# Attention with q/k norm, then a squared-ReLU feed-forward: pair 0's exponentials ahead of the weights, half of q's norm product on ScalarE, one weight tick moved to the next stage, the last pair summed from its parts

## The chip, the core and the metric

The kernel runs on one core of a Trainium2 chip. The metric is the device time of one execution in microseconds (us), lower is better. Times of the kernel before and after are medians of several executions; the profile is that of one execution.

The engines have their own queues of instructions and wait for each other by semaphores: TensorE (PE in the profile; its weight loads are PEld), VectorE (DVE), ScalarE (ACT), GpSimd (POOL) and SyncE (SP, which issues the transfers).

## The reference

Eight batches, twelve heads, 448 positions, head size 64. q and k are normalised by their root mean square and multiplied by gains; then softmax attention; the heads' outputs side by side make 3584 tokens of 768, which go through a feed-forward of 768 to 2048 to 768 with a squared ReLU.

```python
def rmsnorm(x, g):
    rms = np.sqrt(np.mean(x * x, axis=-1, keepdims=True) + 1e-06)
    return x / rms * g
q_n, k_n = (rmsnorm(q, g_q), rmsnorm(k, g_k))
scores = scale * np.matmul(q_n, k_n.transpose(0, 1, 3, 2))
scores = scores - np.max(scores, axis=-1, keepdims=True)
attn = np.exp(scores)
attn = attn / (np.sum(attn, axis=-1, keepdims=True) + 1e-09)
attn_out = np.matmul(attn, v)
# x: (B, H, S, D) -> (B*S, H*D)
h = x @ w_in
r = np.maximum(h, 0.0)
return ((r * r) @ w_out)
```

The weights arrive as float64 and are turned into float32 on the chip.

## The kernel before

A pair is two heads of one batch. There are 48; the work goes in four spans of two batches (twelve pairs). The first twelve pairs' attention runs alone (attention_alone); the later spans' attention runs among the second products of the span before. The two products of the feed-forward are block products with seven multiplications in place of eight, whose sums and differences of weight blocks (S1 to S4) are made once, during attention_alone and the first product of span 0, and written to DRAM.

Each engine's instructions come in the order in which this program writes them (manual_schedule). So each statement below also says what stands behind what in a queue.

**The norm of a pair.** Squares on ScalarE, sums on VectorE, the power -1/2 and the product with q on GpSimd. k is not multiplied: its factor goes into the exponential as a scale. normalise_in_turn is the form for pair 1, with q and k apart and the product on VectorE.

```python
def normalise_in_turn(nc, raw, sq, rstd, mhalf, between=lambda: None):
    SP, _, n = rstd.shape
    for s in range(2):
        nc.scalar.activation(sq[:, s], raw[:, s], AF.Square)  # L332
        nc.vector.tensor_reduce(rstd[:, s], sq[:, s].rearrange("p (n d) -> p n d", n=n), AX, ALU.add)  # L333
        nc.vector.tensor_scalar(rstd[:, s], rstd[:, s], float(n) / sq.shape[2], 1e-6, ALU.mult, ALU.add)  # L334
        nc.gpsimd.tensor_tensor(rstd[:, s], rstd[:, s], mhalf[:SP, 0:n], ALU.pow)  # L335
        if s == 0:
            between()
            nc.vector.tensor_tensor(sq[:, 0].rearrange("p (j h d) -> p h j d", j=n // 2, h=2),  # L338
                                    raw[:, 0].rearrange("p (h j d) -> p h j d", j=n // 2, h=2),
                                    rstd[:, 0].rearrange("p (h j) -> p h j ()", h=2)
                                    .to_broadcast([SP, 2, n // 2, sq.shape[2] // n]), ALU.mult)

def norm(i):
    if i >= NAT:
        squares(i)
        return norm_by_squares(i)
    raw, sq = (places_of(qk, i, n)[:SP] for n in range(2))
    rstd = rstds[i] = small.tile([SP, 2, 2 * NJ], F32, tag="rstd", name="rstd", bufs=4)
    normed[i] = sq[:, 0], raw[:, 1]
    if i == 1:
        return normalise_in_turn(nc, raw, sq, rstd, mhalf)
    nc.scalar.activation(sq, raw, AF.Square)  # L698
    nc.vector.tensor_reduce(rstd, sq.rearrange("p s (n d) -> p s n d", d=D), AX, ALU.add)  # L699
    nc.vector.tensor_scalar(rstd, rstd, 1.0 / D, 1e-6, ALU.mult, ALU.add)  # L700
    flat = rstd.rearrange("p s n -> p (s n)")
    nc.gpsimd.tensor_tensor(flat, flat, mhalf[:SP, 0:4 * NJ], ALU.pow)  # L702
    nc.gpsimd.tensor_tensor(sq[:, 0].rearrange("p (j h d) -> p h j d", j=NJ, h=2),  # L704
                            raw[:, 0].rearrange("p (h j d) -> p h j d", j=NJ, h=2),
                            rstd[:, 0].rearrange("p (h j) -> p h j ()", h=2).to_broadcast([SP, 2, NJ, D]),
                            ALU.mult)
```

**One pair's scores, values and total.** The exponentials are on ScalarE (L759). The sum over keys is made by adding the first three tiles of exponentials on VectorE (add_up), and multiplying that sum and the fourth tile with ones on TensorE (total_of). finish divides, and combine_x makes the sums of xT that the first product takes as operands (its second group reads xC[:, 1]).

```python
def transpose(i, s, n):
    pt = bank("pt", n)
    for j in range(NJ):
        nc.tensor.transpose(pt[:, j * SP:(j + 1) * SP], normed[i][s][:, j * P:(j + 1) * P], ident[:SP, :SP])  # L742
    if s:
        nc.scalar.copy(qkT[:, i % 2, s], pt)  # L744
    else:
        nc.scalar.activation(qkT[:, i % 2, s], pt, AF.Copy, scale=gains[:, 0:1])  # L746
# ...
def scores(i, c):
    at = i % 2 if i < NAT else 0
    sc = ps_s.tile([SP, 2, 512], F32, tag="s", name="sc")
    for h in range(2):
        rows = slice(h * D, (h + 1) * D)
        nc.tensor.matmul(sc[:, h, 0:S], qkT[rows, at, 1, c * SP:(c + 1) * SP], qkT[rows, at, 0, :],  # L754
                         start=True, stop=True)
    pr = probs[i, c] = places[(NJ * i + c) % len(places)][:SP]
    if i < NAT:
        for h in range(2):
            nc.scalar.activation(pr[:, h], sc[:, h, 0:S], AF.Exp, scale=rstds[i][:, 1, 2 * c + h:2 * c + h + 1])  # L759
# ...
def add_up(i, c):
    acc = acc_of(i)[:SP]
    nc.vector.tensor_tensor(acc, probs[i, 0] if c == 1 else acc, probs[i, c], ALU.add)  # L769
# ...
def values(i, chunks=range(NJ)):
# ...
        pavs[i] = ps_o.tile([P, S], F32, tag="o", name="pav") if i >= NAT or i % 2 == 0 else bank("pav", 1)
    for c in chunks:
        for h in range(2):
            nc.tensor.matmul(pavs[i][h * D:(h + 1) * D, :], vs[i][:, h, c, :], probs[i, c][:, h, :],  # L810
                             start=(c == 0), stop=(c == NJ - 1))
def total_of(i):
    tots[i] = ps_o.tile([P, S], F32, tag="t", name="tot")
    for n, pr in enumerate((acc_of(i)[:SP], probs[i, NJ - 1])):
        for h in range(2):
            nc.tensor.matmul(tots[i][h * D:(h + 1) * D, :], sums["ones"], pr[:, h, :],  # L819
                             start=(n == 0), stop=(n == 1))
# ...
def finish(i):
    b, hp = divmod(i, NPAIR)
    pav, factors = pavs.pop(i), xT[:, b % 2, hp]
    x = factors
    if i < NAT:
        turned, factors = sums["turned"], sums["factors"]
        few = small.tile([P, S // 32], F32, tag="few", name="few")
        nc.vector.transpose(turned, tots.pop(i))  # L832
        nc.vector.reciprocal(few, turned.rearrange("p (g r) -> p g r", r=32)[:, :, 0])  # L833
        nc.vector.transpose(factors.rearrange("p (g r) -> p g r", r=32),  # L834
                            few.rearrange("p g -> p g ()").to_broadcast([P, S // 32, 32]))
        x = x.rearrange("d (p j) -> d j p", j=NJ)
        pav, factors = (t.rearrange("d (j p) -> d j p", j=NJ) for t in (pav, factors))
    nc.vector.tensor_tensor(x, pav, factors, ALU.mult)  # L839
# ...
def combine_x(i):
# ...
    if b % 2:
# ...
        else:
            n = hp - HC
            sub(xC[:, 1, n], xT[:, 1, hp], xC[:, 0, n], ALU.subtract)  # L852
            sub(xC[:, 2, n], xT[:, 0, hp], xC[:, 1, n], ALU.subtract)  # L853
            sub(xT[:, 1, n], xT[:, 1, hp], xT[:, 1, n], ALU.subtract)  # L854
```

**The loop over the first twelve pairs.** At every yield the caller puts in steps of the weights' preparation.

```python
def attention_alone():
    for i in range(NAT):
        more = i + 1 < NAT
        if i + 3 < NAT:
            load(i + 3)
        scores(i, 0)
        scores(i, 1)
        if i + 2 < NAT:
            norm(i + 2)
        elif not more:
            norm(NAT)
            load(NAT + 2)
        add_up(i, 1)
        yield
        if i:
            transpose(i + 1, 1, 0) if more else None
            values(i - 1, (2, 3))
            total_of(i - 1)
            transpose(i + 1, 0, 0) if more else None
            finish(i - 1)
        load_v(i + 1)
        yield
        scores(i, 2)
        scores(i, 3)
        if i == 0:
            transpose(1, 0, 0)
            transpose(1, 1, 1)
        values(i, (0, 1))
        yield
        add_up(i, 2)
        if i:
            combine_x(i - 1)
        if NAT <= i + 3 < NAT + 2:
            load(i + 3)
        yield
    values(i, (2, 3))
    total_of(i)
    finish(i)
    combine_x(i)
```

**The weights' preparation.** It goes in ticks of four steps, one tick for each of 32 blocks of weights (and three to run out): ScalarE takes L580 and L596, VectorE L593, L598 and L603, GpSimd L568 (two) and, at every second tick, L574 (four). A block's words lie in one of six places: one in the stage, two in the part of gT that is free till the end of the first product, three buffers of their own.

```python
WORDS, BLOCKS, EXPS, LAST = 6, 2, 4, 31
EARLY, ALL = 4 * 13, 4 * (2 * NFC + 3)
# ...
def place_of(n):
    return n % WORDS if n < LAST else 3
# ...
def load_words(t, done):
    while loaded[0] <= t + 3 and all(
            place_of(m) != place_of(loaded[0]) for m in range(max(done, 0), loaded[0])):
        load_w(loaded[0])
        loaded[0] += 1
def prepare(t):
# ...
    def value(n, half):
# ...
            _, eu, low, _ = parts(n)
            nc.gpsimd.tensor_tensor(*[x.bitcast(I32) for x in (dst, low[:, part], eu[:, part])], ALU.add)  # L568
# ...
    def total(n, dst, x, y, op):
        if there(n) and n % 2:
            nc.gpsimd.tensor_tensor(*[blocks_of(n)[:, i] for i in (dst, x, y)], op)  # L574
# ...
    def unsigned(n):
# ...
            nc.scalar.activation(e, high.bitcast(F32), AF.Abs)  # L580
# ...
    if t == 0:
        unsigned(0)
    n = t - 3
    if there(n) and n % 2:
        c = n % NFC // 2
        dst = w1s[c] if n < NFC else w2s[:, c // 4, :, c % 4]
        nc.sync.dma_start(dst.rearrange("k p m -> p k m"), blocks_of(n)[:, 0:7])
        written[0] = n + 1
    if there(t) and doubles:
        e, eu, low, high = parts(t)
        nc.vector.tensor_scalar(e, e, 2.0 ** -15, 1.875 * 2.0 ** 16, ALU.max, ALU.min)  # L593
    yield
    if there(t) and doubles:
        nc.scalar.activation(low.bitcast(I32), low, AF.Copy, scale=2.0 ** -29)  # L596
        bits = banks.get("bits", eu)
        nc.vector.tensor_scalar(bits, eu, 3, 0x3FFFFFF8, ALU.logical_shift_left, ALU.bitwise_and)  # L598
    if t < 3:
        load_words(t, t - 1)
    yield
    if there(t) and doubles:
        nc.vector.scalar_tensor_tensor(eu, high, 0xC0000000, bits, ALU.bitwise_and, ALU.bitwise_or)  # L603
    total(t - 2, S3, A11, A21, ALU.subtract)
    total(t - 2, S4, A12, S2, ALU.subtract)
    value(t - 1, 0)
    yield
    unsigned(t + 1)
    value(t - 1, 1)
    total(t - 1, S1, A21, A22, ALU.add)
    total(t - 1, S2, S1, A11, ALU.subtract)
    load_words(t, t - 1)
    yield
```

**What calls it.** Ticks are spread over attention_alone up to EARLY steps, and over the first product of span 0 up to ALL.

```python
with tc.tile_pool(name="words", bufs=2) as spare["pool"]:
    for _ in range(2):
        load_w(loaded[0])
        loaded[0] += 1
    load(2)
    norm(1)
# ...
        weights(4)
        for u, _ in enumerate(attention_alone()):
            weights(min(EARLY, 8 + (EARLY - 8) * (u + 1) // (4 * NAT - 4)))
            if u == 4 * NAT - 6:
                load_blocks(5)
    with tc.tile_pool(name="first_product", bufs=2, reuse_waits="tile") as work:
        for u, _ in enumerate(first_product(work, 0)):
            # ...
            weights(min(ALL, EARLY + (ALL - EARLY) * (u - 1) // (N1 - 6)))
```

## Time and profile before

| | |
|---|---|
| median of 3 executions | 1406.07 us (1404.28 to 1408.61) |
| span of the profiled execution | 1404.7 us |
| PE busy | 1377.9 us, 98% of the span |
| DVE, ACT, POOL busy | 813.5 us (58%), 420.3 us (30%), 591.0 us (42%) |
| start of the first product of span 0 | 139.89 us |
| transfers | 188.78 MB, mean 134 GB/s |

The page's slices cut the span into 40 equal parts; each digit is the busy share in tenths. A row of the table of stretches gives the stretch, its length, and each engine's busy us with its number of instructions, then the granted TensorE clock, the transfers' share and their rate. A row of the waits says which engine and line waited for which, the total in us, how often, and the longest. A row of a timeline gives start, duration, engine, line, operation, output and input; in square brackets stands how long the engine had been idle and for whom it waited.

### The profile page before, as it was taken

How to read it: one execution, taken by the hardware profiler on the slowest of the kernel's cores; microseconds unless marked ns; L12 is line 12 of the kernel's file. 1: busy time of each engine (PE TensorE's matmuls, PEld its weight loads, DVE VectorE, ACT ScalarE, POOL GpSimd, SP SyncE). 2: the span in 40 equal slices, each digit the busy share in tenths (PEclk: the TensorE clock that was granted, in tenths of full speed). 3: DMA queues.
4: the chain of work that ended last, by engine and by line, in shares of the span. 5: the costliest groups of instructions: out<-in, count | busy, mean ns of one | idle time of the engine just before them, and what ended most of it. 6: DMA issues, size and time to landing. Idle time of an engine off the chain costs nothing.

```text
span 1404.7 us, 14407 instructions
## 1 busy us (share of the span) xinstructions
PE 1377.9 (98%) x4422; PEld 636.9 (45%) x4422; DVE 813.5 (58%) x1402; ACT 420.3 (30%) x620; POOL 591.0 (42%) x400
## 2 busy tenths in 40 slices
PE   7998999999999999999999999999999999999998
PEld 3333445444444455544444455444444445554554
DVE  6999677489876333576777523457777633332111
ACT  7775565433332011233332011232333201110000
POOL 7999687544453022554344112445435302221000
PEclk9999999999999999999999999999999999999999
DMA  8767899645655433345576333345565333333443
GB/s 242 215 192 199 278 378 327 184 106 119 128 115 119 102 85 90 100 109 123 108 138 121 98 94 90 98 104 112 119 128 105 96 98 90 86 90 101 106 110 72
DMA packets 430914, 188.78 MB, mean 134 GB/s; under 512 B 277484, under 2 KB 428780, under 8 KB 430828
## 3 DMA queue, kind: packets, MB, share of 16 engines
q1 hardware_dynamic: 421228, 179.05, 49.2%
q10 hardware_dynamic: 9472, 8.72, 2.4%
q8 instruction: 37, 0.61, 0.2%
q14 instruction: 49, 0.40, 0.1%
q0 software_dynamic: 128, 0.00, 0.0%
HBM read 154.54 MB, written 33.16 MB: 134 GB/s over the span
## 4 chain that ended last, share of the span: by engine, by line
PE 91%; POOL 4%; DVE 2%; DMA 1%; issue 1%; ACT 1%; SPq 0%; POOLq 0%; DVEq 0%
PE ps L1036 37%; PE pa L989 10%; PE pd L989 10%; PE pc L989 10%; PE sc L754 9%; PE pav L810 9%; PE pb L989 5%; POOL rstd L702 1%; POOL gC L568 1%; DMA sw<-w1s 1%; DVE gT L769 0%; DMA gT<-in_moe_w_in_dram 0%; POOL qk L704 0%; PE tot L819 0%; POOL gC L574 0%
## 5 line engine op out<-in xcount | busy, mean ns | idle before, releaser
L1036 PE MATMUL ps<-gT,sw 128*128 128x448 f32 x768 | 299.2, 542 | 0.8 <-POOL gT L966 0.8
L724 POOL TENSOR_TENSOR half<-half,mhalf 128x28 f32<-128x28 f32 x36 | 173.8, 4827 | 259.7 <-DVE half L723 227.7
L1036 PE MATMUL ps<-gC,sw 128*128 128x448 f32 x576 | 225.2, 542 | 0.0
L966 POOL TENSOR_TENSOR gT<-gT 128x448 f32<-128x448 f32 x96 | 93.5, 976 | 311.9 <-ACT gT L962 311.9
L1036 PEld LDWEIGHTS ps<-gT,sw 128*128 128x128 f32 x768 | 143.9, 190 | 151.0 <-issue 147.5
L761 ACT ACTIVATE pr<-sc 112x896 f32<-112x896 f32 x120 | 104.8, 915 | 296.4 <-PE sc L754 205.6
L754 PE MATMUL sc<-qkT 64*112 64x448 f32 x768 | 171.8, 567 | 6.1 <-ACT gT L759 3.9
L1036 PEld LDWEIGHTS ps<-gC,sw 128*128 128x128 f32 x576 | 108.0, 190 | 112.3 <-issue 111.4
L989 PE MATMUL pa<-xT,sw 128*128 128x448 f32 x384 | 156.2, 543 | 0.4 <-DMA sw<-w1s 0.4
L962 ACT ACTIVATE gT<-gT 128x448 f32<-128x448 f32 x96 | 55.3, 576 | 309.6 <-DVE gT L1004 309.6
L754 PEld LDWEIGHTS sc<-qkT 64*112 64x112 f32 x768 | 61.6, 173 | 104.7 <-issue 80.5
L989 PEld LDWEIGHTS pa<-xT,sw 128*128 128x128 f32 x384 | 73.4, 192 | 73.8 <-issue 73.3
L810 PE MATMUL pav<-pr,vt 112*64 112x448 f32 x480 | 100.2, 547 | 0.0
L726 POOL TENSOR_TENSOR qk<-qk,half 128x448 f32<-128x448 f32 x72 | 84.9, 1198 | 2.8
L769 DVE TENSOR_TENSOR acc<-acc,pr 112x896 f32<-112x896 f32 x60 | 68.1, 1135 | 19.1 <-ACT pr L761 16.2
L1004 DVE TENSOR_TENSOR gT<-z,pd 128x448 f32<-128x448 f32 x32 | 19.8, 620 | 101.2 <-PE pd L989 101.2
L989 PE MATMUL pd<-xT,sw 128*128 128x448 f32 x192 | 77.9, 542 | 0.0
L989 PE MATMUL pb<-xC,sw 128*128 128x448 f32 x192 | 77.4, 539 | 0.0
L989 PE MATMUL pc<-xC,sw 128*128 128x448 f32 x192 | 77.4, 539 | 0.0
L989 PE MATMUL pd<-xC,sw 128*128 128x448 f32 x192 | 77.4, 539 | 0.0
L989 PE MATMUL pc<-xT,sw 128*128 128x448 f32 x192 | 77.4, 539 | 0.0
L574 POOL TENSOR_TENSOR gC<-gC 128x384 f32<-128x384 f32 x64 | 72.2, 1145 | 2.5
(120 smaller groups left out, 1564.2 us busy)
## 6 DMA issues: line engine op xcount, KB each, us to landing
sw<-w1s SPq DMA_DIRECT2D x224, 192.0 KB, 2.3
sw<-w2s SPq DMA_DIRECT2D x168, 256.0 KB, 3.2
w1s<-gC SPq DMA_DIRECT2D x8, 1344.0 KB, 7.5
w2s<-gC SPq DMA_DIRECT2D x8, 1344.0 KB, 8.4
out_dram<-osb SPq DMA_DIRECT2D x184, 56.0 KB, 1.9
qk<-in_q_dram SPq DMA_DIRECT2D x144, 56.0 KB, 2.9
qk<-in_k_dram SPq DMA_DIRECT2D x144, 56.0 KB, 2.7
vt<-in_v_dram SPq DMA_DIRECT2D x72, 112.0 KB, 2.8
```

Of the source, the lines that this page charges most:

```text
L574: nc.gpsimd.tensor_tensor(*[blocks_of(n)[:, i] for i in (dst, x, y)], op)
L724: nc.gpsimd.tensor_tensor(half, half, mhalf, ALU.pow)
L726: nc.gpsimd.tensor_tensor(qkn[:, s], raw[:, s], half[:, s * NG:(s + 1) * NG].rearrange("p g -> p g ()").to_broadcast([P, NG, 32]), ALU.mult)
L754: nc.tensor.matmul(sc[:, h, 0:S], qkT[rows, at, 1, c * SP:(c + 1) * SP], qkT[rows, at, 0, :], start=True, stop=True)
L761: nc.scalar.activation(pr, sc[:, :, 0:S], AF.Exp)
L769: nc.vector.tensor_tensor(acc, probs[i, 0] if c == 1 else acc, probs[i, c], ALU.add)
L810: nc.tensor.matmul(pavs[i][h * D:(h + 1) * D, :], vs[i][:, h, c, :], probs[i, c][:, h, :], start=(c == 0), stop=(c == NJ - 1))
L962: nc.scalar.activation(g, src, AF.Relu)
L966: nc.gpsimd.tensor_tensor(g, g, g, ALU.mult)
L989: nc.tensor.matmul(ps, stream[n + i][:, c], rhs[:, c], start=first and c == 0, stop=c == HC - 1, skip_group_check=not first)
L1004: add(g, x, ps, ALU.add)
L1036: nc.tensor.matmul(ps, stream[n][:, c % 4], rhs_of[i][:, c], start=c == 0, stop=c == HF - 1)
```

## The change

It has several parts, all but one in the first twelve pairs:

- Pair 0: its four exponentials (and pair 1's transposes) come ahead of all steps of the weights and of pair 2's norm, so that ScalarE doesn't stand behind the weights' first transfers. Its yields fall to one. load(2) goes ahead of the first two loads of words.
- In norm, the product of q for the first of the two heads goes to ScalarE, as four copies with a scale; GpSimd keeps the second head. This is to relieve GpSimd. Pair 2 takes normalise_in_turn, as pair 1 does.
- In the loop, the transpose of the next pair's k, the values and the total of the pair before come ahead of the norm of the pair after next.
- EARLY falls from 13 ticks to 12: one tick moves from attention_alone into the first product. The steps are spread anew.
- The words have seven places in place of six, four of them buffers of their own; few and p1 get one buffer in place of two to make room.
- The last pair's total takes the third and fourth exponentials directly, without the last add_up.

```diff
# ...
-    WORDS, BLOCKS, EXPS, LAST = 6, 2, 4, 31
-    EARLY, ALL = 4 * 13, 4 * (2 * NFC + 3)
+    WORDS, BLOCKS, EXPS = 7, 2, 4
+    EARLY, ALL = 4 * 12, 4 * (2 * NFC + 3)
# ...
-    def place_of(n):
-        return n % WORDS if n < LAST else 3
     def words_of(n):
-        place = place_of(n)
+        place = n % WORDS
         if place == 0:
# ...
     def load_words(t, done):
-        while loaded[0] <= t + 3 and all(
-                place_of(m) != place_of(loaded[0]) for m in range(max(done, 0), loaded[0])):
+        while loaded[0] <= t + WORDS - 3 and loaded[0] < max(done, 0) + WORDS:
             load_w(loaded[0])
             loaded[0] += 1
# ...
         raw, sq = (places_of(qk, i, n)[:SP] for n in range(2))
         rstd = rstds[i] = small.tile([SP, 2, 2 * NJ], F32, tag="rstd", name="rstd", bufs=4)
         normed[i] = sq[:, 0], raw[:, 1]
-        if i == 1:
+        if i <= 2:
             return normalise_in_turn(nc, raw, sq, rstd, mhalf)
         nc.scalar.activation(sq, raw, AF.Square)
         nc.vector.tensor_reduce(rstd, sq.rearrange("p s (n d) -> p s n d", d=D), AX, ALU.add)
# ...
         flat = rstd.rearrange("p s n -> p (s n)")
         nc.gpsimd.tensor_tensor(flat, flat, mhalf[:SP, 0:4 * NJ], ALU.pow)
-        nc.gpsimd.tensor_tensor(sq[:, 0].rearrange("p (j h d) -> p h j d", j=NJ, h=2),
-                                raw[:, 0].rearrange("p (h j d) -> p h j d", j=NJ, h=2),
-                                rstd[:, 0].rearrange("p (h j) -> p h j ()", h=2).to_broadcast([SP, 2, NJ, D]),
-                                ALU.mult)
+        src = raw[:, 0].rearrange("p (h j d) -> p h j d", j=NJ, h=2)
+        dst = sq[:, 0].rearrange("p (j h d) -> p h j d", j=NJ, h=2)
+        for j in range(NJ):
+            nc.scalar.activation(dst[:, 0, j], src[:, 0, j], AF.Copy, scale=rstd[:, 0, j:j + 1])
+        nc.gpsimd.tensor_tensor(dst[:, 1], src[:, 1],
+                                rstd[:, 0, NJ:].rearrange("p j -> p j ()").to_broadcast([SP, NJ, D]), ALU.mult)
# ...
         tots[i] = ps_o.tile([P, S], F32, tag="t", name="tot")
-        for n, pr in enumerate((acc_of(i)[:SP], probs[i, NJ - 1])):
+        parts = [acc_of(i)[:SP]] + [probs[i, c] for c in range(2 if i + 1 == NAT else 3, NJ)]
+        for n, pr in enumerate(parts):
             for h in range(2):
                 nc.tensor.matmul(tots[i][h * D:(h + 1) * D, :], sums["ones"], pr[:, h, :],
-                                 start=(n == 0), stop=(n == 1))
+                                 start=(n == 0), stop=(n + 1 == len(parts)))
     def finish(i):
# ...
             turned, factors = sums["turned"], sums["factors"]
-            few = small.tile([P, S // 32], F32, tag="few", name="few")
+            few = small.tile([P, S // 32], F32, tag="few", name="few", bufs=1)
             nc.vector.transpose(turned, tots.pop(i))
             nc.vector.reciprocal(few, turned.rearrange("p (g r) -> p g r", r=32)[:, :, 0])
             nc.vector.transpose(factors.rearrange("p (g r) -> p g r", r=32),
# ...
                 load(i + 3)
             scores(i, 0)
             scores(i, 1)
+            if i == 0:
+                transpose(1, 1, 1)
+                scores(0, 2)
+                scores(0, 3)
+                transpose(1, 0, 0)
+                add_up(0, 1)
+                add_up(0, 2)
+                norm(2)
+                load_v(1)
+                values(0, (0, 1))
+                yield
+                continue
+            if more:
+                transpose(i + 1, 1, 0)
+            values(i - 1, (2, 3))
+            total_of(i - 1)
             if i + 2 < NAT:
                 norm(i + 2)
             elif not more:
# ...
                 load(NAT + 2)
             add_up(i, 1)
             yield
-            if i:
-                transpose(i + 1, 1, 0) if more else None
-                values(i - 1, (2, 3))
-                total_of(i - 1)
-                transpose(i + 1, 0, 0) if more else None
-                finish(i - 1)
+            if more:
+                transpose(i + 1, 0, 0)
+            finish(i - 1)
             load_v(i + 1)
             yield
             scores(i, 2)
             scores(i, 3)
-            if i == 0:
-                transpose(1, 0, 0)
-                transpose(1, 1, 1)
             values(i, (0, 1))
             yield
-            add_up(i, 2)
-            if i:
-                combine_x(i - 1)
+            if more:
+                add_up(i, 2)
+            combine_x(i - 1)
             if NAT <= i + 3 < NAT + 2:
                 load(i + 3)
             yield
# ...
                     nc.tensor.matmul(ps, stream[n + i][:, c], rhs[:, c], start=first and c == 0,
                                      stop=c == HC - 1, skip_group_check=not first)
                 if i == A11:
-                    p1 = work.tile([P, S], F32, tag="p1", name="p1")
+                    p1 = work.tile([P, S], F32, tag="p1", name="p1", bufs=1)
                     nc.scalar.copy(p1, ps)
# ...
     with tc.tile_pool(name="words", bufs=2) as spare["pool"]:
+        load(2)
         for _ in range(2):
             load_w(loaded[0])
             loaded[0] += 1
-        load(2)
         norm(1)
         with tc.tile_pool(name="first", bufs=2, reuse_waits="tile") as work:
# ...
             sums["turned"], sums["factors"] = (g[:, 0:S] for g in free[2 * NJ + 2:2 * NJ + 4])
             sums["ones"] = work.tile([SP, D], F32, tag="ones", name="ones", bufs=1)
             nc.vector.memset(sums["ones"], 1.0)
-            weights(4)
             for u, _ in enumerate(attention_alone()):
-                weights(min(EARLY, 8 + (EARLY - 8) * (u + 1) // (4 * NAT - 4)))
-                if u == 4 * NAT - 6:
+                weights(min(EARLY, 4 + (EARLY - 4) * u // (4 * NAT - 7)))
+                if u == 4 * NAT - 9:
                     load_blocks(5)
```

## The prediction, made before the change was run

> **What bounds the kernel now.** I read the page's slices first, to find where TensorE is not full; then the table of stretches, the waits between 23 and 124 us, and the timelines of each engine at the two ends and for one pair in the middle.
>
> ```profile
> PE   7998999999999999999999999999999999999998
> POOL 7999687544453022554344112445435302221000
> ```
>
> A slice is 35 us. TensorE (PE) is full from the fifth slice on; what can be won lies in the first 140 us, the attention of the first twelve pairs. The first product starts at 139.89 us.
>
> ```profile
> core 0: us, PE busy (x) PEld busy (x) DVE busy (x) ACT busy (x) POOL busy (x), PEclk, DMA share, GB/s
> 80.00:95.00 15.00, 14.03 (x74) 5.30 (x72) 13.82 (x18) 12.33 (x22) 14.77 (x11) 1.00 0.92 278
> 95.00:110.00 15.00, 12.93 (x70) 4.96 (x68) 13.96 (x18) 10.43 (x19) 14.84 (x9) 1.00 0.59 175
> ```
>
> In that stage GpSimd (POOL) is busy all the time, 14.8 of 15 us; ScalarE (ACT) has room. The waits between 23 and 124 us name the op (total us, times, longest):
>
> ```profile
> ACT qkT L746 <- PE pt L742: 21.7, 10, 3.8
> PE pt L742 <- POOL qk L704: 6.9, 8, 1.4
> ```
>
> So once a pair TensorE waits some 1 us for q's norm product (L704), last link of a GpSimd queue that is a whole pair behind. One pair's norm, through three engines:
>
> ```profile
> 96.00 1.07 ACT L698 ACTIVATE qk<-qk 112x1024 f32<-112x1024 f32 x1
> 97.11 1.22 DVE L699 TENSOR_REDUCE rstd<-qk 112x16 f32<-112x1024 f32 x1 [0.49 <-ACT qk L698]
> 104.51 3.61 POOL L702 TENSOR_TENSOR rstd<-rstd,mhalf 112x16 f32<-112x16 f32 x1
> 108.20 1.04 POOL L704 TENSOR_TENSOR qk<-qk,rstd 112x512 f32<-112x512 f32 x1
> 109.30 0.60 PE L742 MATMUL pt<-ident,qk 112*128 112x112 f32 x4 [0.96 <-POOL qk L704]
> ```
>
> The squares end at 97.07, the power at 108.12: 11 us later. That costs ScalarE nothing now, because nobody on ScalarE asks for the power in this pair. The pairs' first exponentials start at 104.08 and 114.37: a period of 10.3 us, of which GpSimd's work is 10.2 and TensorE's 9.2 (scores 2 x 1.69, values 2 x 1.65, total 1.5, transposes 2 x 0.53).
>
> The two ends:
>
> ```profile
> 9.02 3.08 PE L754 MATMUL sc<-qkT 64*112 64x448 f32 x8 [0.77 <-ACT qkT L383]
> 13.99 0.91 ACT L580 ACTIVATE gC<-gT 128x768 f32<-128x768 f32 x1 [0.69 <-DMA gT<-in_moe_w_in_dram]
> 14.80 2.20 ACT L759 ACTIVATE gT<-sc,rstd 112x448 f32<-112x448 f32 x4
> 130.47 3.23 PE L810 MATMUL pav<-gT,vt 112*64 112x448 f32 x16
> 136.70 3.26 PE L819 MATMUL tot<-gT,ones 112*64 112x448 f32 x8 [3.00 <-DVE gT L769]
> 139.89 3.77 PE L989 MATMUL pa<-xT,sw 128*128 128x448 f32 x6
> ```
>
> At the start the scores are there before 12 us, but the exponentials stand behind a conversion that waits for a weight transfer. At the end the last pair's total waits 3.00 us for its summing on VectorE (DVE), and after it matmuls run at half speed for a while (3.26 against 1.67 for the same eight).
>
> **What the Trainium skill says.** "PSUM — Partial Sum Buffer", section "Engine vs sequencer instructions": "ScalarE/VectorE/GpSimdE queues are strict FIFO." The trace agrees: the exponentials of pair 0, ready by 12 us, started at 14.80, behind L580. "TensorE: Matmul & The Clock Gate", "What's actually happening", says that the array falls to half its clock after an idle window of about 3.4 us and needs as long to return. The trace: after 3.90 us of idleness eight score matmuls took 3.23 us, elsewhere 1.76. "ScalarE: Activation LUTs", "What ACT_TABLE_LOAD costs", gives about 280 ns plus 0.833 ns an element to an instruction with a pointer operand; exponentials of 448 show 635 ns here, 653 by that formula.
>
> **The change, part by part.** Step 1, **the start**. Pair 0's eight exponentials (0.52 us apart, 4.2 us) follow the squares of pair 1 directly: about 10.2 to 15.4, with one 0.53 copy between; then L746 to 16.0, two squares of pair 2 (0.6 each) to 17.2, and only then the first tick's three weight conversions (0.9 each) to 19.8. Pair 1's first exponential starts at 19.8, where the trace has 24.53. The start gains 4.7 us.
>
> Step 2, **half of q's product on ScalarE**. GpSimd loses some 0.5 us a pair, and one tick out of the stage takes off about 0.4 more, so GpSimd stops being the bound (pow 3.5, half product 0.55, weights 4.9: 9 us a pair). But the four copies are written directly behind the squares, on ScalarE, and take the power as their scale. In a strict queue everything behind them, L746 and both later exponentials of the pair, and all of the next pair, stands still until the power is there. The distance of a pair that hid the power is gone. The ring on ScalarE, from one pair's squares to the next:
> - squares 1.07, hand-over 0.03, reduction 1.25 (start to start, L699 to L700), L700 0.2, hand-over 0.08, power 3.4 (3.2 to 3.6 where VectorE did little beside it; GpSimd has nothing queued by then), hand-over 0.07: 6.1
> - four copies of 112x64: from 448 and 768 columns (0.52 and 0.81 start to start) about 0.2 each, an estimate: 0.8
> - L746 0.53, four exponentials 2.08, four more 2.08, L744 0.53: 5.2
> - one tick's conversions, 0.81 and 0.95, at 1.07 ticks a pair: 1.9
>
> The sum is 14.0 us a pair in place of 10.3. TensorE's 9.2 us leave it about 4.5 us idle in one piece, long enough to lose its clock as above; the next scores then come late by some 0.2. I take 14.2. The stall stands in pairs 1 to 9 (norms 3 to 11; norm 2 now goes through VectorE). Pair 2's first exponential: 19.8 + 14.0 = 33.8, and the trace has 33.78, so the first stall eats the whole start. Pair 10's: 33.8 + 8 x 14.2 = 147.4 against 114.37, **33.0 us later**.
>
> Step 3, **pairs 10 and 11** have no such norm. The ninth tick's rest and GpSimd's backlog are gone, so pair 10 goes at TensorE's speed, 9.5 in place of 10.75: 1.2 gained.
>
> Step 4, **the last total**. It takes the fourth and third exponentials directly: four more matmuls (0.8 us), but it needs no second summing. What remains ahead is the bank that pair 10's total leaves at 133.71. From 133.7, twelve matmuls at full clock (2.4) end at 136.2 where the trace has 139.96; and the first product's first group takes 2.3 in place of 3.6. Its second group, now at 143.50, needs xC of the last pair: L832 to L852 take 3.3 us after the total (139.99 to 143.35), which is just covered. Gain 4.7.
>
> Step 5, **the tick moved**. 92 steps instead of 88 go into the first product. The number of word loads before it is the same (up to block 15 either way); one write of 1344 KB moves in. The transfers there are full (0.98 to 1.05 of the share from 155 to 230 us), while the extra buffer lets words come earlier and one wait of 0.44 us stands there now. I put +0.5. The other single buffers (few, p1) I put at nothing.
>
> Sum: 1406.1 + 33.0 - 1.2 - 4.7 + 0.5 = 1433.7; I say **1433 us**.
>
> **The rivals.** (a) The purpose comes true: the copies don't hold ScalarE up, the pair falls to TensorE's 9.3 to 9.6, saving some 7 us over nine pairs, the start 4.7, the end 5: about 1390. For it: ScalarE waits 21.7 us in the stage for nothing useful. Against: those idle pieces come at L746, behind the squares, and are only 2.2 us each, while squares to power needs 5 at least. Only an order other than the program's could save it, and every queue in this trace follows the program. (b) As (a), but the moved tick costs more than the 4 us of GpSimd work that it frees, since transfers there are full: 1.3 MB at 350 GB/s is 3.8 us, so 1395 to 1405. For it the 0.44 us wait; against it the deeper words. (c) My ring, but with TensorE cold for all of its scores, transposes and sums: then e1 and L744 wait too, 0.5 to 0.8 a pair: 1437 to 1440.
>
> **Range and chances.** The ring's error is 0.5 us a pair, over eight pairs 4; the start and the end may each be off by 2, the product by 3; together about 6, and rival (c) adds above: 1419 to 1443. The 2% line is at 1434.2, as good as at my number. Slower by over 2%: 0.47, within 2%: 0.50 (here lie (a) and (b) with some 0.06), faster by over 2%: 0.03.
>
> **What would show it.** Right: among the waits of 23 to 160 us a new one, ScalarE's copy in norm on GpSimd's power, some 5 us nine times; pair period about 14 us; POOL's share falling to two thirds of the stage; PEclk under 1 in it; the first product starting near 167 us. The power should follow L700 at once. Step 1: first exponential near 10.2. Step 4: no wait of the last total for a summing. Wrong: if the pairs come every 9 to 10 us, the strict queue isn't what holds them, and the time is near 1390. If the period is right but the total isn't, look at the first product for waits on sw.

## The result, and the profile after

The changed kernel takes **1447.26 us** against 1406.01 us: slower, ratio 1.0292 (95% interval 1.0274 to 1.031). The prediction said 1433, between 1419 and 1443. It had the cause in kind, gave a slowdown of over 2% a chance of 0.47, and was 14 us short.

Three rows of the page's slices, then two waits from 18 to 160 us (total us, times, longest). The changed kernel's line numbers differ from those of the code above: L702 is ScalarE's copy, L693 the squares, L697 the power, L756 the exponentials, L751 the scores.

```profile
PE   7767899999999999999999999999999999999998
POOL 5665688854454112445435302354455302221000
PEclk9887999999999999999999999999999999999999
```

```profile
ACT qk L702 <- POOL rstd L697: 53.4, 9, 6.2
PE sc L751 <- ACT gT L756: 38.2, 9, 6.3
```

GpSimd (POOL) is no longer full in the first slices. It fell to five to six tenths because it waits in the ring too: 40.1 us in all, its power for VectorE's sums (L695). ScalarE's copies wait for the power nine times, 5.9 us each, and TensorE's scores wait for ScalarE's exponentials nine times. In three of the first four slices the granted clock is only seven or eight tenths. The stage of the stalled pairs in the table of stretches:

```profile
31.50:154.20 122.70, 90.81 (x385) 33.63 (x385) 71.36 (x91) 72.15 (x138) 76.89 (x47) 0.83 0.42 125
```

TensorE works 90.8 of 122.7 us, at a granted clock of 0.83, and no engine is full: they wait for each other in a ring. One turn of it, from the timelines of ScalarE, VectorE, GpSimd and TensorE:

```profile
36.38 1.07 ACT L693 ACTIVATE qk<-qk 112x1024 f32<-112x1024 f32 x1
43.36 1.06 ACT L702 ACTIVATE qk<-qk,rstd 112x64 f32<-112x64 f32 x4 [5.90 <-POOL rstd L697]
44.33 0.61 ACT L743 ACTIVATE qkT<-pt,gains 128x448 f32<-128x448 f32 x1
44.84 0.89 ACT L591 ACTIVATE gT<-gT 128x768 int32<-128x768 uint32 x1
45.62 2.19 ACT L756 ACTIVATE gT<-sc,rstd 112x448 f32<-112x448 f32 x4
...
48.71 1.16 ACT L756 ACTIVATE gT<-sc,rstd 112x448 f32<-112x448 f32 x2
50.20 1.16 ACT L756 ACTIVATE gT<-sc,rstd 112x448 f32<-112x448 f32 x2 [0.34 <-PE sc L751]
51.25 0.53 ACT L741 COPY qkT<-pt 128x448 f32<-128x448 f32 x1
51.66 1.08 ACT L693 ACTIVATE qk<-qk 112x1024 f32<-112x1024 f32 x1
```

```profile
38.74 0.17 DVE L695 TENSOR_SCALAR rstd<-rstd 112x16 f32<-112x16 f32 x1
38.83 1.08 DVE L766 TENSOR_TENSOR gT<-gT 112x896 f32<-112x896 f32 x1
```

```profile
39.00 4.33 POOL L697 TENSOR_TENSOR rstd<-rstd,mhalf 112x16 f32<-112x16 f32 x1 [7.58 <-DVE rstd L695]
```

```profile
46.82 3.33 PE L751 MATMUL sc<-qkT 64*112 64x448 f32 x8 [4.38 <-ACT gT L756]
```

From squares to squares 15.28 us. GpSimd had been idle for 7.58 us before the power, so nothing of its own work held the power up.

The two ends, which were to gain, did. At the start, ScalarE's pair 0 and pair 1 in the changed kernel, then pair 1 in the kernel before:

```profile
10.03 2.21 ACT L756 ACTIVATE gT<-sc,rstd 112x448 f32<-112x448 f32 x4
...
18.55 2.27 ACT L756 ACTIVATE gT<-sc,rstd 112x448 f32<-112x448 f32 x4
```

```profile
24.53 2.21 ACT L759 ACTIVATE gT<-sc,rstd 112x448 f32<-112x448 f32 x4 [0.35 <-PE sc L754]
```

At the end, TensorE in the changed kernel:

```profile
174.68 2.42 PE L817 MATMUL tot<-gT,ones 112*64 112x448 f32 x12
177.04 2.52 PE L998 MATMUL pa<-xT,sw 128*128 128x448 f32 x6
180.41 2.49 PE L998 MATMUL pb<-xC,sw 128*128 128x448 f32 x6 [0.85 <-PE pa L998]
...
191.63 4.19 PE L998 MATMUL pd<-xC,sw 128*128 128x448 f32 x6 [1.96 <-DMA sw<-w1s]
```

Pair 1's first exponential comes 6 us earlier, and the last total waits for nothing. The last line is new: the first product waits for its sixth block of weights.

### The profile page after: what moved, and what is told of

Its sections match the earlier page's. It is cut to its first block, busy times and chain, and to the rows that moved or that the text cites. A ratio compares the mean times of both kernels' runs of the same rounds, so it can differ in the third digit from the quotient of the medians.

```text
span 1446.2 us, 14396 instructions
## 1 busy us (share of the span) xinstructions
PE 1393.8 (96%) x4426; PEld 641.8 (44%) x4426; DVE 811.0 (56%) x1404; ACT 428.8 (30%) x657; POOL 585.0 (40%) x400
## 4 chain that ended last, share of the span: by engine, by line
PE 88%; POOL 6%; issue 3%; DVE 1%; ACT 1%; DMA 1%; SPq 0%; POOLq 0%; ACTq 0%; DVEq 0%
PE ps L1045 36%; PE pd L998 10%; PE pc L998 10%; PE pa L998 10%; PE sc L751 9%; PE pav L807 9%; PE pb L998 5%; POOL rstd L697 3%; POOL gC L569 1%; POOL gC L563 1%; POOL qk L703 1%; PE tot L817 0%; DMA sw<-w1s 0%; PE idle L374 0%; DMA vt<-in_v_dram 0%
## 5 line engine op out<-in xcount | busy, mean ns | idle before, releaser
L751 PE MATMUL sc<-qkT 64*112 64x448 f32 x768 | 183.0, 597 | 39.0 <-ACT gT L756 38.2
L751 PEld LDWEIGHTS sc<-qkT 64*112 64x112 f32 x768 | 64.1, 182 | 141.0 <-issue 81.4
```

## The experiments

Times are medians; ratios are to the kernel before on the same chip. Places in time come from one profiled execution each. The kernel before itself ranges from 1401 to 1409 us, so a single profile says little about 1 or 2 us. The length of a pair is the mean from pair 2's first exponential to pair 10's. The length of the first product is the time from its second group to the second product's first instruction.

**Undoing the half product.** Everything of the change but ScalarE's copies:

```diff
-for j in range(NJ): nc.scalar.activation(dst[:, 0, j], src[:, 0, j], AF.Copy, scale=rstd[:, 0, j:j + 1])
-nc.gpsimd.tensor_tensor(dst[:, 1], ...)
+nc.gpsimd.tensor_tensor(sq[:, 0]..., raw[:, 0]..., rstd[:, 0]..., ALU.mult)   # both heads, as before
```

> The changed kernel, but q's norm product of both heads is GpSimd's again (one instruction, as before); all other parts of the change stay. Theory (ScalarE's copies, in a strict queue, wait for the power, and that ring of 15.3 us sets the pair): no wait of ScalarE on GpSimd's power; the pairs fall back to GpSimd's 10.0 to 10.4 us; pair 1's first exponential stays near 18.6 us, pair 10's comes near 111 (156.1 in the changed kernel); time about 1400, range 1394 to 1406. Rival (the new order of the loop, transposes and totals ahead of the norm, or the tick spread anew, costs the pairs their time): pairs stay above 13 us and the time above 1430.

Measured: 1405.28 us, ratio 1.0 (0.9989 to 1.001). Pairs of 10.5 us (10.1 in the kernel before), no wait of ScalarE on the power. All of the slowdown goes with the copies. The other parts together are worth nothing in time. Pair 10's scores came at 108.27 where they had come at 113.17. But pair 10 itself took 14.3 us, behind a product on GpSimd that took 3.90 us in place of 1.04; the totals waited 6.2 us for summing; and the first product took 128.66 us in place of 126.75.

**The half product alone**, put into the kernel before:

```diff
-nc.gpsimd.tensor_tensor(sq[:, 0]..., raw[:, 0]..., rstd[:, 0]..., ALU.mult)
+for j in range(NJ): nc.scalar.activation(dst[:, 0, j], src[:, 0, j], AF.Copy, scale=rstd[:, 0, j:j + 1])
+nc.gpsimd.tensor_tensor(dst[:, 1], ...)
```

> The kernel before, with one part of the change alone: the first head's product by ScalarE's four copies. Theory: the ring stands here too, in ten pairs (norms 2 to 11), and longer, since in the old order the copy of the next pair's k stands behind the stall and q's transposes need its bank: 15.3 to 16.3 us a pair; time 1450 to 1465. Rival (the half product relieves GpSimd, and another part does the harm): 1398 to 1404, with pairs of about 9.7 us.

Measured: 1479.51 us, ratio 1.053 (1.0506 to 1.0553); 17.5 us a pair. Both are more than expected. In the old order the copy of the next pair's k (L746) stands behind the stall as well, q's transposes wait for it, and ScalarE once more for them. From ScalarE's timeline of this run:

```profile
79.00 1.07 ACT L707 ACTIVATE qk<-qk,rstd 112x64 f32<-112x64 f32 x4 [5.95 <-POOL rstd L702]
79.97 0.51 ACT L746 COPY qkT<-pt 128x448 f32<-128x448 f32 x1
81.65 0.64 ACT L748 ACTIVATE qkT<-pt,gains 128x448 f32<-128x448 f32 x1 [1.16 <-PE pt L744]
```

So the new order of the loop, which the change also brings, saves some 2 us a pair of a harm that another part does.

**The power in two**, q's eight columns first:

```diff
-nc.gpsimd.tensor_tensor(flat, flat, mhalf[:SP, 0:4 * NJ], ALU.pow)
+for s in range(2):
+    nc.gpsimd.tensor_tensor(rstd[:, s], rstd[:, s], mhalf[:SP, 0:2 * NJ], ALU.pow)
```

> The changed kernel with GpSimd's power cut into q's eight columns first and k's eight after, so that the copies wait for half as much. Theory (all of the ring's length passes into the pair's period): the wait before the copies falls by about 2 us, from 5.9 to 4, in nine pairs, so the time falls by 16 to 20 us, to 1427 to 1432, and the period to 13.3. Rival (the period is set by TensorE being cold, or by scores that wait for their buffer, and the power is partly hidden): under 8 us are won, 1439 to 1447.

Measured: 1431.78 us, ratio 1.0197 (1.0173 to 1.0221). The wait before the copies falls from 5.9 to 4.6 us (41.3 in nine pairs), the pair from 15.3 to 13.6. What leaves the ring leaves the period. GpSimd makes the same sixteen columns, only in two pieces, so it is not the amount of its work that binds.

**VectorE quiet during the power.** A tiny copy makes VectorE wait for the power:

```diff
+nc.vector.tensor_copy(quiet, rstd[:, 0, 0:1])   # behind norm; never read
```

> The changed kernel with one tiny VectorE copy of a column of the power behind norm, so that VectorE stands still while GpSimd makes the power, and does its summing and finishing after it. Theory (the power takes 4.3 us in place of the 3.2 to 3.6 of the kernel before because VectorE's adds and transposes keep GpSimd from SBUF): the power falls to 3.2 to 3.4 us, ScalarE's wait before the copies from 5.9 to 4.9, and the time by 7 to 10 us, to 1437 to 1441. Rival (the power takes 4.3 us by itself, when GpSimd comes from idleness): it stays at 4.3, and the time stays or grows.

Measured: 1441.09 us, ratio 1.0262 (1.0245 to 1.0279).

```profile
66.40 2.91 POOL L697 TENSOR_TENSOR rstd<-rstd,mhalf 112x16 f32<-112x16 f32 x1 [7.76 <-DVE rstd L695]
...
69.34 0.15 DVE L706 COPY quiet<-rstd 112x1 f32<-112x1 f32 x1 [3.02 <-POOL rstd L697]
...
69.41 3.49 DVE L768 TENSOR_TENSOR gT<-gT 112x896 f32<-112x896 f32 x1
...
69.95 2.00 POOL L563 TENSOR_TENSOR gC<-words,gC 128x384 int32<-128x384 int32 x2
```

The power takes 2.91 us in all nine pairs, in place of 4.32: it was VectorE that made it long, not a start from idleness. By the profile it was worth 6.3 us (the first product's second group at 174.08, not 180.41) and not more. One reason is in the lines: VectorE's adds, pushed behind the power, now meet GpSimd's weights, and this one takes 3.49 us in place of 1.08.

The timelines say which of VectorE's work it is. In the changed kernel an add begins 0.17 us ahead of every one of these powers, and another operation follows it directly. These two end 1.4 to 1.8 us after the power's start, and the power is 1.2 to 1.6 us longer than 2.91. What VectorE begins later, while the power runs, need not cost anything: in the run that undid the half product, a power of 2.95 us (at 68.15) had an add of 1.09 us wholly inside it.

**TensorE kept warm** with added matmuls that nobody reads:

```diff
 values(i, (0, 1))
+if i + 2 < NAT:
+    idle = ps_o.tile([P, S], F32, tag="t", name="idle")
+    for _ in range(5):
+        nc.tensor.matmul(idle, qkT[:, i % 2, 0, 0:P], qkT[:, i % 2, 1], start=True, stop=True)
```

> The changed kernel with five idle matmuls (128x128 by 128x448, into the free bank of the totals, never read) behind the values of pairs 1 to 9, so that TensorE is not idle for more than 1 to 2 us while ScalarE waits. They are added work. Theory (ScalarE's ring sets the pair, TensorE's low clock adds only the half microsecond by which the scores come late to the exponentials): eight scores take 1.76 us again in place of 3.3, the exponentials' waits of 0.34 vanish, the period falls from 15.3 to 14.8 and the time by 3 to 6 us, to 1441 to 1444. Rival (the low clock is the main cost of the stalls): the time falls by over 15 us.

Measured: 1442.65 us, ratio 1.0269 (1.0252 to 1.0287). Pairs of 14.8 us, as expected. Filling TensorE's idle time with work that means nothing makes the kernel faster by 3 to 5 us (3.2 by the ratios, 4.6 by the medians); the low clock's part of the ring is that half microsecond a pair. The scores behind the stall, which took 3.33 us in the turn shown above, take 2.05.

**The same copies, later in the queue.** GpSimd's half stays where it is:

```diff
 def norm(i):
-    for j in range(NJ): nc.scalar.activation(...)
+    later[i] = dst, src, rstd
 for i in range(NAT):
+    rest_of_product(i + 1)          # the four copies of the pair before
     if i + 3 < NAT: load(i + 3)
```

> The changed kernel with the same four copies on ScalarE, only written later: at the start of the next pair's turn, ahead of its load, in place of directly behind the squares. Nothing is left out. Theory (it is the place in the queue, not the work): the wait on the power falls from 53 us to under 10 in all, the pairs come every 9.6 to 10.3 us, time 1394 to 1403. Rival (ScalarE's added work or the shared power itself is what costs): little changes, above 1435.

Measured: 1417.03 us, ratio 1.009 (1.0069 to 1.0112). The wait on the power falls from 53.4 to 5.3 us, and 30 of the 41 us are back:

```profile
ACT qk L711 <- POOL rstd L697: 5.3, 4, 1.8
```

But the pairs take 12.0 us, not 10, so something else holds them. VectorE, GpSimd, TensorE in this run:

```profile
76.36 5.36 DVE L773 TENSOR_TENSOR gT<-gT 112x896 f32<-112x896 f32 x1
```

```profile
75.99 0.92 POOL L702 TENSOR_TENSOR qk<-qk,rstd 112x256 f32<-112x256 f32 x1
76.88 1.95 POOL L569 TENSOR_TENSOR gC<-gC 128x384 f32<-128x384 f32 x2
78.79 1.97 POOL L563 TENSOR_TENSOR gC<-words,gC 128x384 int32<-128x384 int32 x2
```

```profile
81.78 3.25 PE L824 MATMUL tot<-gT,ones 112*64 112x448 f32 x8 [3.63 <-DVE gT L773]
```

The second summing, 1.08 us in the kernel before, takes 5.36 and ends 1 us after a row of five GpSimd products, which kept their speed. The totals wait for such summings 17.8 us in all. This fits what the Trainium skill says in "SBUF — State Buffer", "SBUF: two separate sides": VectorE's operations with two SBUF inputs and GpSimd share one pair of ports as an exclusive lock, and "the other fully blocks". The powers that grew behind an add begun ahead of them fit it as well. One point differs: the page has the lock held for a whole instruction, but the power of 2.95 us named above ran with an add wholly inside it, and neither was longer for it by more than 0.04 us. That the lock is the reason is not shown by a run.

**Later totals too**, as a cure for that wait:

```diff
-values(i - 1, (2, 3)); total_of(i - 1); norm(i + 2) ... finish(i - 1) ... scores(i, 2); scores(i, 3)
+values(i - 1, (2, 3)); norm(i + 2) ... scores(i, 2); scores(i, 3); total_of(i - 1); finish(i - 1)
```

> As the run with the copies a pair later, and in addition the total and the finishing of the pair before stand behind the pair's last scores in place of ahead of the norm (TensorE waited there 17.8 us in all for VectorE's summing, itself up to 5.4 us long beside GpSimd), and the load of pair 14 comes in the first product. Nothing is left out. Theory (these two waits are what kept that run at 1417): pairs every 9.5 to 10.2 us, no wait of the total, time 1392 to 1402, below the kernel before. Rival (VectorE's summing, starved by GpSimd, just holds up something else): 1408 to 1418.

Measured: 1415.98 us, ratio 1.0086 (1.0069 to 1.0103). A miss: 1392 to 1402 was expected. The totals' wait falls to 3.2 us, but the copies wait 17.5 us for the power again: at the head of the next pair they are only some 4 us of ScalarE's work behind their squares, and the ring closes anew there.

**Copies a whole period later, totals without the summing.** The copies stand behind the next pair's squares, the loads behind them, and every total takes the third and fourth exponentials directly:

```diff
     norm(i + 2)
+    rest_of_product(i + 1)
+    if i + 3 < NAT: load(i + 3)
-    add_up(i, 2)
-parts = [acc_of(i)[:SP]] + [probs[i, c] for c in range(2 if i + 1 == NAT else 3, NJ)]
+parts = [acc_of(i)[:SP]] + [probs[i, c] for c in range(2, NJ)]
```

> The changed kernel with ScalarE's copies of a pair behind the squares of the next pair (a whole period after their own squares), the loads of q and k behind them, and every pair's total taken from the third and fourth exponentials directly, without the second summing (0.8 us more of TensorE, 1.1 us less of VectorE a pair). Nothing is left out. Theory (wait on the power, and VectorE's summing starved by GpSimd, are what held the two versions before this at 1416): neither wait is there, pairs every 10.0 to 10.4 us, time 1396 to 1404. Rival (other waits come up, such as q's and k's later loads): 1408 and more.

Measured: **1402.04 us**, ratio 0.9973 (0.9963 to 0.9984), faster than both kernels. The wait on the power is 0.6 us in all, and in the table of stretches TensorE is full:

```profile
55.00:70.00 15.00, 15.00 (x80) 5.83 (x78) 14.72 (x17) 13.96 (x28) 14.58 (x10) 1.00 0.86 263
```

**The same totals with the whole product on GpSimd**, that is, the half product undone as in the first experiment, and of the last one only the direct totals:

```diff
-    add_up(i, 2)
-parts = [acc_of(i)[:SP]] + [probs[i, c] for c in range(2 if i + 1 == NAT else 3, NJ)]
+parts = [acc_of(i)[:SP]] + [probs[i, c] for c in range(2, NJ)]
```

> The changed kernel with the whole product on GpSimd, and every pair's total taken directly, as in the run beside this one. Theory (GpSimd's 10 us a pair is the bound of that version, and the 6 us of waits of totals for summing lie partly beside it): the waits of the totals vanish, VectorE keeps GpSimd from SBUF less, time 1399 to 1404, a little below the kernel before. Rival (the four more matmuls a pair put TensorE at 10.0 us, nothing is won): 1404 to 1408.

Measured: 1402.08 us, ratio 0.9979 (0.9972 to 0.9987). As good: in both runs most pairs take 10.01 us, which is TensorE's time with the four added matmuls. With totals direct, the half product on ScalarE brings nothing; the summing taken off VectorE does.

**Late copies with the summing kept**, against the version of 1402.04 us:

```diff
+    if more: add_up(i, 2)
-parts = [acc_of(i)[:SP]] + [probs[i, c] for c in range(2, NJ)]
+parts = [acc_of(i)[:SP]] + [probs[i, c] for c in range(2 if i + 1 == NAT else 3, NJ)]
```

> The version with ScalarE's copies behind the next pair's squares, but with the second summing of each pair on VectorE kept (only the last pair's total direct), so that TensorE has 9.2 us a pair in place of 10.0. Nothing is left out. Theory (with the wait on the power gone, GpSimd's 9.4 us and TensorE's 9.2 are the bounds, if VectorE's summing isn't starved): pairs of 9.4 to 10.0 us, time 1394 to 1402. Rival (VectorE's summing is starved by GpSimd's bursts as in the run with the copies a pair later): totals wait some 2 us every other pair, pairs of 10.3 to 11.5, time 1404 to 1416.

Measured: 1412.97 us, ratio 1.0058 (1.0045 to 1.0071); the rival held. The totals wait 12.9 us for a summing that is starved again (up to 5.38 us).

**The last total alone**, in the kernel before:

```diff
-for n, pr in enumerate((acc_of(i)[:SP], probs[i, NJ - 1])):
+parts = [acc_of(i)[:SP]] + [probs[i, c] for c in range(2 if i + 1 == NAT else 3, NJ)]
+for n, pr in enumerate(parts):
-    add_up(i, 2)
+    if more: add_up(i, 2)
```

> The kernel before with one part of the change alone: the last pair's total takes the third and fourth exponentials directly and the last summing is left out. Theory (its gain in the changed kernel, 4.8 us at the second group of the first product, is its own, but the first product gives part of it back, since the weights of its sixth block and its words come no earlier): second group of the first product at 139 to 140 us in place of 143.5, first product 1 to 3 us longer, time 1402 to 1405. Rival (nothing is given back, the first product only suffers from the moved tick): 1401 to 1402.

Measured: 1403.55 us, ratio 0.999 (0.9983 to 0.9996): 1.3 us. In its profile the second group begins at 138.34, and the first product takes 126.36 us, so nothing was given back there, against the theory. But that was the kernel's quickest execution, and its pairs ran 1.8 us ahead before the last total. By the medians, the part is worth about a quarter of what step 4 gives it.

**The first product.** It takes 126.75 us before and, with its second group at 180.41 as shown above, 131.24 after. The kernel before, then the changed one:

```profile
143.50 2.42 PE L989 MATMUL pb<-xC,sw 128*128 128x448 f32 x6
270.25 1.77 PE L1036 MATMUL ps<-gT,sw 128*128 128x448 f32 x4
```

```profile
311.65 1.77 PE L1045 MATMUL ps<-gT,sw 128*128 128x448 f32 x4
```

SyncE's queue stands behind the load of pair 14, which waits for GpSimd's product of pair 12, and the sixth block is asked for at 186.04 us, needed at 189.7. Three runs: that load moved to the first product's tenth group, the thirteenth tick put back, and both:

```diff
-    norm(NAT); load(NAT + 2)
+    norm(NAT)                        # load(NAT + 2) at u == 9 of the first product
```

```diff
-EARLY, ALL = 4 * 12, ...
+EARLY, ALL = 4 * 13, ...
```

> The changed kernel with the load of q and k of pair 14 moved from pair 11's turn to the tenth group of the first product, so that SyncE's queue doesn't stand behind GpSimd's product of pair 12 when the first product asks for its sixth block of weights. Theory: the wait of 1.96 us on sw and the cold matmuls after it (4.19 in place of 2.42) vanish; first product shorter by 3 to 4 us; time 1443 to 1444.5. Rival (the transfers are full there because of the tick that was moved in): the wait moves or stays, time 1446 to 1448.

> The changed kernel with the thirteenth tick back in the attention (13 ticks early, as before). Theory (the first product is longer by 4.5 us than it was, because one more tick of weights stands in it): in the stalled pairs the tick costs under 1 us, since GpSimd is idle for 5 us a pair, and the first product gets 2 to 4.5 us shorter; time 1443 to 1446. Rival (the first product's loss comes from its earlier start against the loads and norms that it waits for, not from the tick): 1446.5 to 1449.

> The changed kernel with both edits to the first product that were tried singly: thirteen ticks early again, and the load of pair 14 in the tenth group of the first product. From the first product's second group to the second product's first, the kernel before takes 126.75 us, the changed kernel 131.24, with the tick back 129.93, with the load moved 130.66. Theory (the held load starves the sixth block, and the moved tick fills the transfers so that the load, moved, starves others): with both it falls to 126.5 to 127.5, the two together doing what neither does; time 1442.5 to 1444. Rival (a third thing, such as the words' places, costs there): 129 or more, time over 1445.

| run | us | ratio | first product, us |
|---|---|---|---|
| load moved | 1448.79 | 1.0319 (1.0302 to 1.0336) | 130.66 |
| tick back | 1446.27 | 1.0294 (1.0277 to 1.031) | 129.93 |
| both | 1445.10 | 1.0303 (1.0284 to 1.0321) | 127.76 |

None of the three reached the time that its theory gave. With the load moved, the wait at the sixth block is gone, but others on sw and on VectorE come in its place, as the rival said. With both edits the stage is 3.5 us shorter in the profile, but the ratios don't tell the runs apart. Nor does the stage: in eight other runs that leave it as the change made it, it took 128.1 to 130.4 us, so a single 127.76 or 131.24 proves little. Put into the version of 1402.04 us, the same two diffs were no help:

> The version with the copies behind the next squares and every total direct (1402), with the thirteenth tick back in the attention and the load of pair 14 in the first product. Theory (GpSimd has room in its pairs, 13.5 of 15 us busy, and the first product returns to 126.5 us from 128.8): pairs stay at 10.03 us, time 1399 to 1401. Rival (the tick makes GpSimd the bound of the pairs again): the pairs lose 1 to 3 us, time 1401 to 1404.

Measured: 1402.47 us, ratio 0.9988 (0.9981 to 0.9995), first product 129.82, against 128.82 without them.

Two things do go through all profiles. Those with twelve ticks have TensorE wait for VectorE in this stage, 0.4 to 1.6 us, and those with thirteen don't. Those with the new words wait for sw, 0.3 to 3.2 us, those with the old words 0.4 at most. The stage takes 126.4 to 126.8 us in the three runs with the old words, and 127.8 to 131.3 in the fourteen with the new. So the division of that loss stays **open**: neither the words' places nor the single buffer of p1, which the first product uses, was tried alone.

## Why the prediction failed

**What held.** Step 2's mechanism: the four copies tie ScalarE's strict queue to the power in the same pair. Undoing them gives all back, moving them gives most back, shortening the power shortens the pair. The stall stands in nine pairs, as said, and rivals (a) and (b) are out. So is (c): a pair's second scores run at full speed again (1.76 us at 39.03), and its exponentials wait only 0.34 us. Step 1 was right in kind and 1.2 us too small. Some 0.5 us of that was a slip in its sum: from 10.2, 4.2 us of exponentials and a copy of 0.53 end at 14.9, not at 15.4.

**The step that failed is step 2's sum, the ring of 14.2 us a pair.** It measured 15.3 from pair 2 to pair 10. Term by term, from the turn shown:

| term | predicted | measured |
|---|---|---|
| squares to the start of the power | 2.63 | 2.62 |
| power and hand-over | 3.47 | 4.36 |
| four copies | 0.8 | 0.97 |
| L743, L741, eight exponentials | 5.2, and 0.2 for the cold scores | 5.53 |
| the tick's conversions | 1.9 | 1.80 |

The power is the mis-sized term: 0.89 of the 1.08 us. I took 3.4 us, "where VectorE did little beside it". The changed kernel starts the power when VectorE has just begun its add; it takes 4.14 to 4.55 us there, and 2.91 with VectorE quiet. Nor was the reading of the old trace right: VectorE worked through most of those powers too, but what it had begun before them ended within 0.9 us. And the trace of before shows one power at whose start things stood as in the changed kernel, with an add begun 0.17 us ahead, and it took 4.14:

```profile
19.31 1.08 DVE L769 TENSOR_TENSOR gT<-gT 112x896 f32<-112x896 f32 x1
```

```profile
19.48 4.14 POOL L702 TENSOR_TENSOR rstd<-rstd,mhalf 112x16 f32<-112x16 f32 x1 [3.59 <-DVE rstd L700]
```

Over eight pairs the ring cost 9.0 us more than predicted, and the first stall 0.9; the start took 1.2 back. That makes 41.7 us at pair 10's first exponential, not 33.0.

**Step 3 and step 4** together gave 4.8 us, not 5.9: pair 10 took 10.06 us, not 9.5, and the first product's second group waits 0.85 us, where I had called its operand xC "just covered". By my own figures it wasn't: 3.3 us after the total, against a first group of 2.3. Nor is xC what it waits for. It begins at 180.41, 1.0 us before pair 11's part of xC (L850) is written:

```profile
179.34 0.97 DVE L837 TENSOR_TENSOR xT<-pav,gT 128x448 f32<-128x448 f32 x1
180.34 1.08 DVE L850 TENSOR_TENSOR xC<-xT,xC 128x448 f32<-128x448 f32 x1
```

It follows the end of L837 by 0.10 us, and so it does in the runs that undid the half product, with the last total alone and with the copies behind the next squares. In the program, this group takes the bank of pair 11's values, which L837 reads last.

**Step 5** was predicted at +0.5 and measured +4.5 in the profile. In it stand the wait for the sixth block (1.96 us), the slow piece after that wait (4.19 in place of 2.42 us) and a wait for VectorE (0.6 us); which parts of the change cost how much stays open. Sum: 41.7 - 4.8 + 4.5 = 41.4 us, the difference of the two profiles at the second product's start; the medians differ by 41.25.

**The range** was too narrow for a ring: an error in one term comes back in every pair. I allowed 0.5 us a pair for a term that the runs show anywhere from 2.9 to 4.6.

## What to carry to other kernels

Giving part of an overloaded engine's work to an idle one doesn't help if the new instruction waits, in the idle engine's queue, for the last result of the overloaded one: put it where its input is a whole period old. Before you shorten one engine's list, ask which of its results the other engine will now stand still for. When VectorE and GpSimd both work on SBUF, a duration read in one arrangement may not hold in another: look at what the other engine will have begun when the instruction starts. For the power here that made the difference between 2.91 and 4.55 us.

## What the runs showed that I had not expected

- The same power of 112x16 takes 2.91 us with VectorE still, and 4.14 to 4.55 us when VectorE has begun an add 0.17 us before it; an add begun while it runs need not lengthen it. The other way, an add of VectorE beside five GpSimd products one behind the other took 5.36 us in place of 1.08.
- Five idle matmuls a pair, added while TensorE would have waited, gained 3 to 5 us, because the scores behind the stall then took 2.05 us and not 3.33.
- Four more matmuls a pair in place of one VectorE add (0.8 us of TensorE against 1.1 of VectorE) gained: the two versions in which it fills TensorE are the quickest, 1402.04 and 1402.08 us.
